# Dense experts in block products: three engines in a fixed order, weights split a pass ahead, GpSimd left out

## The chip, the cores and the metric

One core of a Trainium2 chip runs the whole program. The metric is the time of one execution in microseconds of the device; the median of several runs is compared.

## The reference

Three layers follow each other, all in float32: attention with the queries averaged in pairs, a mixture of 4 dense experts weighted by given probabilities, and a mixture of 8 experts of which each token takes the best one.

```python
def _attn_ref(q, k, v):            # q, k, v: 2 x 8 x 1152 x 64
    q_pool = q.reshape(B, H, S // 2, 2, D).mean(axis=3)
    scores = scale * np.matmul(q_pool, k.transpose(0, 1, 3, 2))
    attn = np.exp(scores - np.max(scores, axis=-1, keepdims=True))
    attn = attn / (np.sum(attn, axis=-1, keepdims=True) + 1e-09)
    return np.matmul(attn, v)
def _moe_ref(x, domain_probs, w1, w2):   # x: 1152 x 512, w1: 4 x 512 x 1024
    p = domain_probs / (domain_probs.sum(-1, keepdims=True) + 1e-09)
    for e in range(E):
        h = np.maximum(x @ w1[e], 0.0)
        out += p[:, e:e + 1] * (h @ w2[e])
def _moe2_ref(x, expert_emb, tau, w1, w2):   # w1: 8 x 512 x 1024
    logits = xn @ en.T / tau                 # x and expert_emb normalised
    expert_idx = np.argmax(logits, axis=1)
    ...
        h = np.maximum(x[mask] @ w1[e], 0.0)
        out[mask] = gate_w[mask, None] * (h @ w2[e])
```

## The kernel before, in words

**Attention** (`attention`, L10 to L236) works through 16 jobs (8 pairs of heads, two parts of the 576 pooled queries each). All its engines follow the order in which the code issues (`tc.manual_schedule()`): scores (L120) and row maxima (matmul L89, VectorE L90, joined at L103), exponentials on ScalarE (L123), sums on GpSimd (L149), the product with v (L155) and the norms (L161 to L172). The first steps (L173 to L188) load k, q and v, and ScalarE issues the loads of v for job 0 itself (L46).

**The dense experts** (`moe1`, L287 to L387) run in eight passes: two halves of 576 tokens (g), four experts (e) each. Every matrix is held as a high part and a remainder, and each product is made of three matmuls. A pass has two phases:

- *Up.* The 512 x 1024 matrix w1 is taken in four units j. A unit multiplies blocks in seven products instead of eight: `unit_w` (L300) loads 512 KB of weights in four pieces, casts 768 columns (ScalarE L308, remainder VectorE L309), forms sums of the blocks with four additions (GpSimd L311 to L314, VectorE for the first two units), and casts 1024 more (L315, L316). The 42 matmuls of a unit, of 288 columns each, go to two kinds of PSUM banks: `ps` collects products one after the other and is copied by ScalarE (`c`, `u`, L334) between them, `py` holds the others (`p` is its copy). VectorE adds (L347, L357), GpSimd adds `u3` (L350), and then ScalarE's relu makes `hh` and VectorE its remainder `hl` (L352, L353).
- *Down.* w2 comes in four pieces of 256 rows, split in high part and remainder (L250, L253). Eight banks (four column blocks d, two groups of tokens of 256 and 320) of 24 matmuls each (L377 to L379) go over `hh` and `hl` of the eight blocks f; VectorE scales the bank by the expert's weight (`prow`), and GpSimd (VectorE for the last expert) adds it to y (L381 to L385).

The order of TensorE in the up phase is that of the code (`manual_schedule` for it alone, L361). All else in `moe1` is placed by the scheduler. `x_sums` (L262) forms the block sums of a half's tokens: for the first half within the last attention jobs, for the second after the up phase of pass 3. The **router** handles ten blocks of tokens (`after`; L484 to L514) whose matmuls use one bank `lr` and one bank `X`; the blocks of each half come at its last expert, two token groups apart (`late`, `flush`). Tables from its counts (matmuls L580, L582) direct the gathers of the routed experts.

**The routed experts** (`moe2`) follow; their weights use buffers of all the pools, and their first matmuls (L700 to L702) stand beside the router's second part.

Of the kernel before, what the change touches and what calls it, by code (L numbers as in the profile page):

```python
# [9 lines left out]
def attention(tc, q, k, v, yr, combos, identF, cc, rp, emb, tau, NJ=16):  # L10

    nc=tc.nc
# [5 lines left out]
    with ExitStack() as ctx:  # L18
# [157 lines left out]
        with tc.manual_schedule():  # L176
# [13 lines left out]
            cb=combos(0,lambda: E1()[:,0:576].rearrange("p (i n) -> p i n",i=2))  # L190
            for g in range(NG):
# [46 lines left out]
NT=10  # L238
# [23 lines left out]
def x_sums(nc, raw, X, tmp):  # L262

    V=nc.vector
    P1,P23,T12,T43=X
    L=[]
    for a in range(2):
        x0,x1=raw[a][:,0],raw[a][:,1]
        lo,hi=slice(0,288),slice(288,576)
        t={}  # L270
        def sub(z,i,i0,i1,t=t):
            def f():
                if z not in t: t[z]=tmp()
                V.tensor_tensor(out=t[z][:,i],in0=i0(),in1=i1(),op=ALU.subtract)
            L.append(f)
        sub(0,0,lambda x0=x0: x0[:,hi],lambda x0=x0: x0[:,lo])
        sub(1,1,lambda x1=x1: x1[:,hi],lambda x0=x0: x0[:,hi])
        sub(0,1,lambda x1=x1: x1[:,hi],lambda t=t: t[0][:,0])
        sub(1,0,lambda x1=x1: x1[:,lo],lambda t=t: t[0][:,1])
        def parts(z,src):  # L280
            L.append(lambda a=a: nc.scalar.copy(z[:,0,a],src()))
            L.append(lambda a=a: V.tensor_tensor(out=z[:,1,a],in0=src(),in1=z[:,0,a].bitcast(F32),op=ALU.subtract))
        parts(T12,lambda t=t: t[0]); parts(T43,lambda t=t: t[1])
        parts(P23,lambda x1=x1: x1.rearrange("p (i n) -> p i n",i=2)); parts(P1,lambda x0=x0: x0[:,lo].rearrange("p (i n) -> p i n",i=1))
    return L

def moe1(tc, pools, ring, hp, tp, psM, psY, yr, X, prow, w1, w2, after, third):  # L287
    nc=tc.nc
    V,G=nc.vector,nc.gpsimd
    ET=mybir.EngineType  # L290
    E=w1.shape[0]
# [4 lines left out]
    late=[]  # L296
    def flush():
        for t in late: after(t)
        late.clear()
    def unit_w(e,j,first):  # L300
# [17 lines left out]
        return [at(wr,0),at(wr,2),at(ws,3),at(wr,1),at(ws,2),at(ws,1),at(ws,0)]  # L318
    for g in range(2):
        for e in range(E):  # L320
            pr=prow(g,e)
            WU=[unit_w(e,j,g==0 and e==0 and j<2) for j in range(4)]
            W2=[load_w(nc,pools,[ring],w2_piece(w2[e],i),('A','V')) for i in range(4)]
            hh=[None]*8; hl=[None]*8
            S=[{} for _ in range(4)]
            def mm(j,i,bank,start,part=(0,6)):
                W=WU[j][i]; z,c=XB[i]
                L=[(W[0][a],z[:,0,a,c]) if m==0 else (W[0][a],z[:,1,a,c]) if m==1 else (W[1][a],z[:,0,a,c]) for a in range(2) for m in range(3)]
                for n,(l,r) in list(enumerate(L))[part[0]:part[1]]:
                    nc.tensor.matmul(bank,l,r,start=start and n==0,stop=n==5,skip_group_check=True)  # L330
            def keep(j,nm,bank):
                if nm=="p1": S[j]['c']=tp.tile([128,2,N],F32,name="c1"); S[j][nm],S[j]["u2"]=S[j]['c'][:,0],S[j]['c'][:,1]
                elif nm!="u2": S[j][nm]=tp.tile([128,N],F32,name=nm)
                nc.scalar.copy(S[j][nm],bank)  # L334
            def p1(j):
                S[j]['X']=psM.tile([128,512],F32,name="ps")[:,0:N]
                mm(j,0,S[j]['X'],True); keep(j,"p1",S[j]['X'])
                for f in (j,j+4):
                    hh[f]=hp.tile([128,576],F32R,name=f"hh{f}"); hl[f]=hp.tile([128,576],F32R,name=f"hl{f}")
            def p5(j):  # L340
                S[j]['Y']=psY.tile([128,512],F32,name="py")[:,0:N]
                mm(j,4,S[j]['Y'],True); keep(j,"p5",S[j]['Y'])
            def p6(j): mm(j,5,S[j]['X'],False); keep(j,"u2",S[j]['X'])
            def p2(j):
                z=psY.tile([128,512],F32,name="py")[:,0:N]
                mm(j,1,z,True)
                V.tensor_tensor(out=S[j]["p1"],in0=z,in1=S[j]["p1"],op=ALU.add)  # L347
            def p7(j):
                mm(j,6,S[j]['X'],False); keep(j,"u3",S[j]['X'])
                G.tensor_tensor(out=S[j]["u3"],in0=S[j]["u3"],in1=S[j]["p5"],op=ALU.add)  # L350
            def low(f,src,cs):
                nc.scalar.activation(out=hh[f][:,cs],in_=src,func=AF.Relu)  # L352
                V.scalar_tensor_tensor(out=hl[f][:,cs],in0=src,scalar=0.0,in1=hh[f][:,cs].bitcast(F32),op0=ALU.max,op1=ALU.subtract)  # L353
# [582 lines left out]
```

## Time and profile before

| | |
|---|---|
| median of 3 runs | 884.47 us (883.15 to 884.5) |
| the profiled execution | 885.35 us, its span 883.6 us |
| mean clock of TensorE | 0.974 of full speed |
| busy: TensorE, VectorE, ScalarE, GpSimd | 803.8, 535.1, 420.5, 393.8 us |

The span is split by stages: attention until about 250.5 us, the eight passes until 729.4, the routed experts until the end. Pass 0 lasts from 250.5 to 317.3, pass 1 to 374.1, pass 2 to 431.7, passes 3 and 4 to 555.9, pass 5 to 612.9, pass 6 to 671.0, pass 7 to 729.4. The share of busy time is a mean over these; which wait ends last is read in each.

### The profile page before, as it was taken

The page shows a single profiled execution, that of the slowest core. Times are in us where ns is not written, and L with a number is a line of the kernel's source. Part 1 is how long each engine was busy: PE and PEld are TensorE (multiplying, and loading weights), DVE is VectorE, ACT ScalarE, POOL GpSimd, SP SyncE. Part 2 cuts the span into 40 slices and gives each one's busy share as a digit, 9 for nine tenths or more (in the row PEclk, how much of TensorE's full clock was granted, in tenths as well). Part 3 has the DMA queues.
Part 4 walks back from the last instruction along what each step waited for, and adds up shares of the span by engine and source line. Part 5 has one row for each costly group of instructions (what it writes and reads, how often), then busy time and mean ns, then how long its engine had stood idle before and what let it go on. Part 6 is the DMA issues. An engine that isn't in the chain of part 4 may idle for free. (4 is left out here: it accounts for less than half of the span.)

```text
span 883.6 us, 16136 instructions
## 1 busy us (share of the span) xinstructions
PE 803.8 (91%) x6067; PEld 700.3 (79%) x6067; DVE 535.1 (61%) x1065; ACT 420.5 (48%) x916; POOL 393.8 (45%) x385
## 2 busy tenths in 40 slices
PE   5999999899967988989889989899798999999996
PEld 3777787677647988978888888889798998877854
DVE  4688888888486346264377565653535848673404
ACT  3466676575745145162273550631614725572524
POOL 4599999878714315355323242353343111330111
PEclk9999999999998999999999999999999999999998
DMA  8532123200044132051231431421313418697991
GB/s 236 143 85 65 27 81 84 29 1 1 2 122 120 49 113 92 3 155 49 68 113 49 120 102 38 133 72 52 106 49 97 154 56 274 236 362 273 394 345 37
DMA packets 101110, 101.32 MB, mean 115 GB/s; under 512 B 28914, under 2 KB 71958, under 8 KB 101024
## 3 DMA queue, kind: packets, MB, share of 16 engines
q1 hardware_dynamic: 97472, 93.71, 33.9%
q0 software_dynamic: 1760, 5.25, 1.7%
q10 hardware_dynamic: 1792, 1.26, 0.5%
q8 instruction: 49, 0.80, 0.4%
q14 instruction: 37, 0.30, 0.1%
HBM read 95.46 MB, written 5.26 MB: 114 GB/s over the span
## 5 line engine op out<-in xcount | busy, mean ns | idle before, releaser
L149 POOL TENSOR_TENSOR es<-es,E 128x512 f32<-128x512 f32 (+1 forms) x108 | 152.9, 1416 | 18.4 <-ACT E L123 10.4
L377 PE MATMUL ps<-hh,w 128*128 128x320 f32 (+1 forms) x512 | 153.3, 301 | 4.0 <-ACT hh L352 4.0
L378 PE MATMUL ps<-hl,w 128*128 128x320 f32 (+1 forms) x512 | 153.8, 300 | 1.5 <-DVE hl L353 1.5
L379 PE MATMUL ps<-hh,w 128*128 128x320 f32 (+1 forms) x512 | 153.2, 300 | 0.0
L330 PE MATMUL ps<-xb,w 128*128 128x288 f32 x576 | 101.8, 314 | 31.5 <-ACT c L334 24.1
L330 PEld LDWEIGHTS ps<-xb,w 128*128 128x128 f32 x576 | 85.7, 199 | 40.4 <-ACT c L334 30.1
L315 ACT CAST w<-st 128x1024 fp32r<-128x1024 f32 x32 | 33.4, 1047 | 173.8 <-issue 130.2
L123 ACT ACTIVATE E<-S 128x320 f32<-128x320 f32 (+1 forms) x288 | 99.7, 411 | 26.4 <-PE S L120 15.6
L330 PE MATMUL py<-xb,w 128*128 128x288 f32 x576 | 99.4, 308 | 11.9 <-ACT w L315 5.9
L377 PEld LDWEIGHTS ps<-hh,w 128*128 128x128 f32 x512 | 98.2, 192 | 4.7 <-ACT hh L352 4.7
L378 PEld LDWEIGHTS ps<-hl,w 128*128 128x128 f32 x512 | 98.4, 192 | 2.4 <-DVE hl L353 2.4
L379 PEld LDWEIGHTS ps<-hh,w 128*128 128x128 f32 x512 | 98.5, 193 | 0.0
L330 PEld LDWEIGHTS py<-xb,w 128*128 128x128 f32 x576 | 86.9, 199 | 14.5 <-ACT p L334 6.5
L253 DVE TENSOR_TENSOR w<-st,w 128x1024 fp32r<-128x1024 f32 x65 | 83.9, 1307 | 23.5 <-ACT w L250 23.0
L90 DVE TENSOR_REDUCE m<-T 128x1 f32<-128x384 f32 x180 | 89.0, 550 | 14.3 <-PE T L89 13.1
L120 PE MATMUL S<-qh,kh 64*128 64x320 f32 (+1 forms) x288 | 86.3, 340 | 1.7 <-ACT E L123 1.7
L120 PE MATMUL S<-qh,kl 64*128 64x320 f32 (+1 forms) x288 | 81.7, 312 | 0.0
L120 PE MATMUL S<-mr,ones 64*128 64x320 f32 (+1 forms) x288 | 78.8, 304 | 0.0
L120 PE MATMUL S<-ql,kh 64*128 64x320 f32 (+1 forms) x288 | 78.3, 305 | 0.0
L155 PE MATMUL O<-E,vn 128*64 128x320 f32 (+1 forms) x576 | 75.7, 409 | 0.0
L250 ACT CAST w<-st 128x1024 fp32r<-128x1024 f32 x65 | 67.5, 1049 | 15.7 <-DMA st<-in_moe_w 8.6
L311 POOL TENSOR_TENSOR st<-st 128x256 f32<-128x256 f32 x30 | 24.4, 814 | 106.1 <-DVE w L309 104.0
(405 smaller groups left out, 1791.8 us busy)
## 6 DMA issues: line engine op xcount, KB each, us to landing
st<-in_moe_w SPq DMA_DIRECT2D x112, 512.0 KB, 5.2
st<-in_moe_w SPq DMA_DIRECT2D x128, 128.0 KB, 3.0
kn<-in_k SPq DMA_DIRECT2D x14, 288.0 KB, 5.0
vn<-in_v SPq DMA_DIRECT2D x14, 288.0 KB, 3.3
qn<-in_q SPq DMA_DIRECT2D x14, 256.0 KB, 4.0
prow<-psc SPq DMA_DIRECT2D x8, 288.0 KB, 4.0
ysc<-ys SPq DMA_DIRECT2D x8, 256.0 KB, 2.1
qn<-in_q SPq DMA_DIRECT2D x14, 64.0 KB, 4.0
```

Source lines behind the costliest of these rows:

```text
L90: nc.vector.tensor_reduce(out=m[:,t,h,c:c+1],in_=s,axis=AX.X,op=ALU.max)
L120: nc.tensor.matmul(s,l[hd],r[hd],start=i==0,stop=i==3)
L123: nc.scalar.activation(out=st['E',g,c][:,h,0:n],in_=s,func=AF.Exp)
L149: nc.gpsimd.tensor_tensor(out=s,in0=st['E',g,0][:,:,0:n] if c==1 else s,in1=st['E',g,c][:,:,0:n],op=ALU.add)
L155: for h in range(2): nc.tensor.matmul(O[HD[h],0:n],vn[:,h,c],st['E',g,c][:,h,0:n],start=c==0,stop=c==NC-1)
L250: if he=='A': nc.scalar.copy(wh,st)
L253: (nc.vector if le=='V' else nc.gpsimd).tensor_tensor(out=wl,in0=st,in1=wh.bitcast(F32),op=ALU.subtract)
L315: nc.scalar.copy(ws[:,0],raw)
L330: nc.tensor.matmul(bank,l,r,start=start and n==0,stop=n==5,skip_group_check=True)
L377: nc.tensor.matmul(po,wh[:,cs],hh[f][:,os],start=(i==0),stop=False)
L378: nc.tensor.matmul(po,wh[:,cs],hl[f][:,os],start=False,stop=False)
L379: nc.tensor.matmul(po,wl[:,cs],hh[f][:,os],start=False,stop=(i==7))
```

## The change

In `moe1` the order of ScalarE and VectorE now follows the code too (`fixed()`), in both phases. The weights of the next pass's units are split in the down phase: `f0` (cast of 768, its remainder, four additions) behind the first bank of each pair, `f1` (cast of 1024, its remainder) behind the second. w2 is loaded and split by column quarters (`down_w`), one in each unit of the up phase. All additions that GpSimd did go to VectorE, but for the four of a unit in the down phase of pass 3, into which the sums of the second half (`x_sums`, now 18 steps in place of 24) are spread. The blocks of the router for the first half are emitted behind pass 3, all five together. The down matmuls take the blocks f in the order 0, 4, 1, 5, 2, 6, 7, 3. The splits of pass 0 are in a fixed order of their own. Some of the pools are allocated ahead of attention; the routed experts have 14 weight buffers in place of 13 and 4 extra stage buffers in place of 5.

```diff
 def moe1(tc, pools, ring, hp, tp, psM, psY, yr, X, prow, w1, w2, after, third):
...
+    fixed=lambda: tc.manual_schedule(engines={ET.PE,ET.Activation,ET.DVE})
...
-    late=[]
-    def flush():
-        for t in late: after(t)
-        late.clear()
-    def unit_w(e,j,first):
+    ORD=[(g,e) for g in range(2) for e in range(E)]
+    WU={}; WD={}
+    def unit_w(n,j,A=V):
...
-        nc.scalar.copy(wr[:,0],raw[:,256:1024])
-        V.tensor_tensor(out=wr[:,1],in0=raw[:,256:1024],in1=wr[:,0].bitcast(F32),op=ALU.subtract)
-        A=V if first else G
-        A.tensor_tensor(out=q[2],in0=q[0],in1=q[2],op=ALU.add)
...
-        nc.scalar.copy(ws[:,0],raw)
-        V.tensor_tensor(out=ws[:,1],in0=raw,in1=ws[:,0].bitcast(F32),op=ALU.subtract)
...
+        def f0():
+            nc.scalar.copy(wr[:,0],raw[:,256:1024])
+            V.tensor_tensor(out=wr[:,1],in0=raw[:,256:1024],in1=wr[:,0].bitcast(F32),op=ALU.subtract)
+            A.tensor_tensor(out=q[2],in0=q[0],in1=q[2],op=ALU.add)
...
+        def f1():
+            nc.scalar.copy(ws[:,0],raw)
+            V.tensor_tensor(out=ws[:,1],in0=raw,in1=ws[:,0].bitcast(F32),op=ALU.subtract)
+        return f0,f1
+    def down_w(n,d):
...
+        nc.sync.dma_start(st.rearrange("p (f c) -> p f c",f=8),w2[e].rearrange("(f p) (d c) -> d p f c",p=128,c=128)[d])
+        w=ring().rearrange("p (l n) -> p l n",l=2)
+        nc.scalar.copy(w[:,0],st)
+        V.tensor_tensor(out=w[:,1],in0=st,in1=w[:,0].bitcast(F32),op=ALU.subtract)
...
-            W2=[load_w(nc,pools,[ring],w2_piece(w2[e],i),('A','V')) for i in range(4)]
...
-                G.tensor_tensor(out=S[j]["u3"],in0=S[j]["u3"],in1=S[j]["p5"],op=ALU.add)
...
-            with tc.manual_schedule(engines={ET.PE}):
...
+        with fixed():
+            for j in range(4):
+                if j==0: p1(0)
...
+                mm(j,4,s['Y'],True); nc.scalar.copy(s['p'],s['Y'])
+                mm(j,5,s['X'],False); nc.scalar.copy(c[:,1],s['X'])
+                if j: out(c21(j-1))
+                down_w(n,j)
...
+                mm(j,1,z,True); V.tensor_tensor(out=c[:,0],in0=z,in1=c[:,0],op=ALU.add)
+                mm(j,2,s['Y'],False,(0,3))
+                mm(j,6,s['X'],False); nc.scalar.copy(s['u'],s['X'])
+                V.tensor_tensor(out=s['u'],in0=s['u'],in1=s['p'],op=ALU.add)
+                if j: out(c1x(j-1))
+                mm(j,2,s['Y'],False,(3,6)); V.tensor_tensor(out=c[:,1],in0=s['Y'],in1=c[:,1],op=ALU.add)
+                if j<3: p1(j+1)
+                else: out(c1x(j))
+                out(c22(j-1 if j<3 else j)) if j else None
+                if j==3: out(c22(2))
+                mm(j,3,s['X'],False)
+            out(c21(3))
...
-                    fs=(0,1,2,4,5,6,3,7)
...
-                        (V if e==E-1 else G).tensor_tensor(out=y,in0=y,in1=t,op=ALU.add)
...
+            for i,f in enumerate((0,4,1,5,2,6,7,3)):
...
+                V.tensor_tensor(out=y,in0=y,in1=t,op=ALU.add)
...
+        with fixed():
+            for i in range(8):
+                d,k=divmod(i,2)
+                bank(d,*PART[g][k])
+                if k==0: pend=unit_w(n+1,d,G if xs else V)
+                pend[k]()
+                for f in xs[i*9//4:(i+1)*9//4]: f()
+        if e==E-1:
+            for t in tiles(0,576): after(t)
+    with fixed():
+        for j in range(4):
+            for f in unit_w(0,j): f()
+    for n in range(len(ORD)): one(n)
...
+            rg=[c2.enter_context(tc.tile_pool(name="ring0",bufs=3,**R,**TW))]
+            sg=[c2.enter_context(tc.tile_pool(name="stage0",bufs=3,**R,**TW))]
             attention(tc,q,k,v,yr,lambda g,tmp: x_sums(nc,yr[g],X,tmp),identF,cc,rp,emb,tau)
...
+            rg.append(c2.enter_context(tc.tile_pool(name="ring1",bufs=6,**R,**TW)))
+            sg.append(c2.enter_context(tc.tile_pool(name="stage1",bufs=1,**R,**TW)))
...
-        sx=c2.enter_context(tc.tile_pool(name="stx",bufs=5,**TW))
...
+        sx=c2.enter_context(tc.tile_pool(name="stx",bufs=4,**TW))
```

How the order moves, at three places.

ScalarE at the start, ahead of job 0. Before (`mr` is the copy of the maxima, `E` the exponentials):

```order
L437 ACTIVATE E,n_243<-E 8x512
L46 DMA vn<-in_v 128x576 x2
L110 CAST mr_277<-T 128x256
L123 ACTIVATE E<-S_287 128x256
L123 ACTIVATE E<-S_289 128x256
L123 ACTIVATE E<-S_313 128x256
```

Now:

```order
L463 ACTIVATE E,n_247<-E 8x512
L46 DMA vn<-in_v 128x576 x2
L310 CAST w<-st 128x768
L110 CAST mr_281<-T 128x256
L317 CAST w<-st 128x1024
L310 CAST w<-st 128x768
L123 ACTIVATE E<-S_294 128x256
L123 ACTIVATE E<-S_296 128x256
```

Three casts of weights stand around the copy of the maxima, ahead of the first exponential. On VectorE a unit's subtractions and additions stand ahead of the maxima of the next job in the same way. Behind attention, VectorE's splits of units 1 to 3 stand in one piece ahead of unit 0's first addition.

ScalarE in an up phase, pass 1. Before (`w` from `st` is a weight cast; `c1`, `p5`, `u3` are copies of PSUM banks):

```order
L352 ACTIVATE hh0_4610<-u3_4647 128x288
L352 ACTIVATE hh4_4612<-c1_4608 128x576
L250 CAST w_4586<-st_4584 128x1024
L334 COPY c1_4665<-ps_4658 128x288
L352 ACTIVATE hh0_4610<-ps_4601 128x288
L334 COPY p5_4686<-py_4679 128x288
L334 COPY c1_4665<-ps_4658 128x288
L334 COPY u3_4712<-ps_4658 128x288
L250 CAST w_4596<-st_4594 128x1024
L352 ACTIVATE hh1_4667<-u3_4712 128x288
L352 ACTIVATE hh5_4669<-c1_4665 128x576
L334 COPY c1_4730<-ps_4723 128x288
```

Now:

```order
L364 COPY u3_4659<-ps_4638 128x288
L346 ACTIVATE hh4_4584<-c1_4581 128x576
L345 COPY c1_4707<-ps_4706 128x288
L346 ACTIVATE hh0_4582<-u3_4595 128x288
L357 COPY p5_4728<-py_4727 128x288
L358 COPY c1_4707<-ps_4706 128x288
L346 ACTIVATE hh1_4640<-ps_4638 128x288
L325 CAST w_4748<-st_4746 128x1024
L364 COPY u3_4729<-ps_4706 128x288
L346 ACTIVATE hh5_4642<-c1_4639 128x576
```

The copies come in the order in which the matmuls make them, with one cast (L325, w2) per unit between them; of the next pass's units only one cast of 768 stands in an up phase, ahead of unit 2 or 3.

TensorE and the router's blocks for the first half. Before, in the down phase of pass 3 (`lr`, `X` are the router's banks, L377 to L379 the down matmuls):

```order
L486 MATMUL X<-identF,y_103 128x128
L377 MATMUL ps<-hh_5748,w 128x320
L378 MATMUL ps<-hl_5749,w 128x320
L379 MATMUL ps<-hh_5748,w 128x320
L377 MATMUL ps<-hh_5805,w 128x320
L378 MATMUL ps<-hl_5806,w 128x320
L484 MATMUL lr<-enT,y_103 128x8
L486 MATMUL X<-identF,y_103 128x128
L379 MATMUL ps<-hh_5805,w 128x320
```

Now, in the up phase of pass 4 (L339 is the up matmul):

```order
L510 MATMUL lr<-enT,y_102 128x8 x4
L512 MATMUL X<-identF,y_102 128x128 x4
L339 MATMUL ps<-xc_101,w 128x288
L512 MATMUL X<-identF,y_102 128x128 x4
L339 MATMUL ps<-xc_101,w 128x288 x5
L339 MATMUL py<-xb_98,w 128x288
L524 LDWEIGHTS ones
L524 MATMUL lr<-oh,ones 128x8
L525 LDWEIGHTS low
L525 MATMUL lr<-oh,low 128x8
L339 MATMUL py<-xb_98,w 128x288 x4
L510 MATMUL lr<-enT,y_102 128x8 x4
```

The blocks moved out of pass 3's down phase, all five to the first 60 up matmuls of pass 4. At the other end of the program, between the last down bank and the first table of the router's second part, 36 matmuls of the routed experts' first layer stand now, and 136 matmuls of the routed experts before.

## Rows read from the trace of the kernel before

**Rows 1.** Busy time by stretch (columns: stretch, its us, busy us of each engine, clock, DMA):
```profile
250.50:317.30 66.80, 53.93 (x359) 51.16 (x357) 37.78 (x59) 25.68 (x47) 18.53 (x20) 0.90 0.33 96
317.30:431.70 114.40, 102.19 (x723) 99.32 (x722) 54.95 (x81) 43.48 (x80) 48.48 (x55) 0.97 0.27 80
431.70:555.90 124.20, 110.95 (x802) 106.99 (x802) 78.58 (x213) 55.01 (x113) 40.02 (x53) 0.96 0.29 87
555.90:671.00 115.10, 103.20 (x727) 99.62 (x726) 54.68 (x81) 44.40 (x82) 48.50 (x55) 0.97 0.27 79
671.00:729.40 58.40, 55.15 (x415) 53.09 (x413) 39.15 (x89) 29.46 (x58) 12.80 (x16) 1.00 0.36 116
374.10:401.10 27.00, 23.00 (x164) 21.70 (x163) 19.01 (x26) 17.32 (x34) 13.19 (x14) 1.00 0.54 148
347.60:374.10 26.50, 26.50 (x200) 26.41 (x199) 8.36 (x14) 4.36 (x8) 9.21 (x12) 1.00 0.08 28
697.60:729.40 31.80, 31.80 (x250) 31.15 (x248) 19.68 (x61) 12.53 (x26) 3.20 (x7) 1.00 0.29 95
729.40:883.60 154.20, 143.16 (x871) 112.05 (x870) 79.21 (x186) 72.96 (x113) 26.48 (x23) 0.97 0.76 275
```

**Rows 2.** Waits of TensorE over the whole span: total us, times, longest:
```profile
PE ps L330 <- ACT c L334: 24.1, 18, 3.1
```

**Rows 3.** Timeline of TensorE, start of pass 2's up phase (start us, us, engine, line):
```profile
374.06 0.96 PE L330 MATMUL ps<-xc,w 128*128 128x288 f32 x6
374.86 0.95 PE L330 MATMUL py<-xb,w 128*128 128x288 f32 x6
```

**Rows 4.** Groups by shape, pass 5's up phase 555.9 to 582.3:
```profile
L253 DVE TENSOR_TENSOR w<-st,w 128x1024 fp32r<-128x1024 f32 x4 | 5.9, 1508 | 0.3 <-ACT w L250 0.3
...
L316 DVE TENSOR_TENSOR w<-st,w 128x1024 fp32r<-128x1024 f32 x3 | 3.7, 1225 | 4.1 <-ACT w L315 4.1
...
L309 DVE TENSOR_TENSOR w<-st,w 128x768 fp32r<-128x768 f32 x3 | 2.9, 955 | 0.3 <-ACT w L308 0.3
...
L353 DVE SCALAR_TENSOR_TENSOR hl<-c,hh 128x576 fp32r<-128x576 f32 x3 | 2.8, 933 | 0.0
...
L347 DVE TENSOR_TENSOR c<-py,c 128x288 f32<-128x288 f32 x4 | 1.8, 450 | 1.8 <-PE py L330 1.8
...
L250 ACT CAST w<-st 128x1024 fp32r<-128x1024 f32 x4 | 4.2, 1043 | 0.0
...
L334 ACT COPY c<-ps 128x288 f32<-128x288 f32 x8 | 3.2, 398 | 0.8 <-PE ps L330 0.7
...
L312 POOL TENSOR_TENSOR st<-st 128x256 f32<-128x256 f32 x3 | 2.6, 870 | 0.2
```

**Rows 5.** Timeline of the start, 13 to 20 us:
```profile
14.61 1.68 ACTq L46 DMA_DIRECT2D vn<-in_v  x2
...
17.03 0.15 DVE L103 TENSOR_REDUCE MM<-m 128x4 f32<-128x12 f32 x1
...
19.17 0.66 ACT L123 ACTIVATE E<-S 128x256 f32<-128x256 f32 x2 [0.78 <-PE S L120]
...
19.49 1.02 DVE L90 TENSOR_REDUCE m<-T 128x1 f32<-128x384 f32 x2 [2.31 <-PE T L89]
```

**Rows 6.** Timeline around the start of pass 0, 246 to 266 us:
```profile
248.58 1.99 ACT L315 CAST w<-st 128x1024 fp32r<-128x1024 f32 x2 [4.70 <-POOL st L314]
...
260.10 0.41 DVE L312 TENSOR_TENSOR st<-st 128x256 f32<-128x256 f32 x1
...
265.21 0.85 PE L330 MATMUL py<-xb,w 128*128 128x288 f32 x2 [5.86 <-ACT w L315]
```

**Rows 7.** Timeline of TensorE in the second router part, 713 to 754 us:
```profile
717.17 0.96 PE L484 MATMUL lr<-enT,y 128*128 128x8 f32 x8
...
720.05 0.96 PE L484 MATMUL lr<-enT,y 128*128 128x8 f32 x8
...
753.18 0.40 PE L580 MATMUL X<-dAm,Bm 128*128 128x30 bf16 x10
```

More of the change, by code (lines that the diff above doesn't have):

```diff
@@ L230, in attention @@
                         av(g,3,NC); norm(g,0)
-                if g>NG//2:
-                    for f in cb[:4]: f()
-                    del cb[:4]
+                if g>=NG//2:
+                    m=2+(g>=NG-2)
+                    for f in cb[:m]: f()
+                    del cb[:m]
             g=NG-1
@@ L265, in x_sums, with sub, f, parts @@
     P1,P23,T12,T43=X
-    L=[]
[L267 to L284, printed above, removed]
+    x=raw.rearrange("p (a k) (i n) -> p k i a n",k=2,i=2)
+    t={}
+    L=[]
+    def sub(n,i0,i1):
+        def f():
+            t[n]=tmp()
+            V.tensor_tensor(out=t[n],in0=i0(),in1=i1(),op=ALU.subtract)
+        return f
+    def parts(z,src):
+        return [lambda: nc.scalar.copy(z[:,0],src()),lambda: V.tensor_tensor(out=z[:,1],in0=src(),in1=z[:,0].bitcast(F32),op=ALU.subtract)]
+    xa=lambda k,i: (lambda: x[:,k,i])
+    ta=lambda n: (lambda: t[n])
+    h1,l1=parts(T12[:,:,0],ta(1)); h2,l2=parts(T12[:,:,1],ta(2)); h4,l4=parts(T43[:,:,0],ta(4)); h3,l3=parts(T43[:,:,1],ta(3))
+    L+=[sub(1,xa(0,1),xa(0,0)),h1,sub(2,xa(1,1),ta(1)),l1,h2,sub(4,xa(1,0),ta(2)),l2,h4,sub(3,xa(1,1),xa(0,1)),l4,h3,l3]
+    for z,k,i in ((P23[:,:,0],1,0),(P23[:,:,1],1,1),(P1[:,:,0],0,0)): L+=parts(z,xa(k,i))
     return L
@@ L389 @@
+    with fixed():
+        for j in range(4):
+            for f in unit_w(0,j): f()
+    for n in range(len(ORD)): one(n)
 NE,NE1=4,3
@@ L481, in block @@
         ts=slice(t,t+1)
-        yt=[yr[g][dc//2][:,dc%2,o:o+n] for dc in range(4)]
+        yt=[yr[g][:,dc,o:o+n] for dc in range(4)]
         lg=psX.tile([128,8],F32,name="lr")[0:n]
@@ L538, in third @@
     def third():
-        two=itertools.cycle([al['x0'],lambda: al['m'](0)])
-        x01=x_parts(nc,psX,"X",dict(x=lambda: next(two)()),res['xs'],2,identF)
+        two=iter([al['x0'](),al['m'](0)])
+        x01=x_parts(nc,psX,"X",dict(x=lambda: next(two)),res['xs'],2,identF)
         x3,x3p=al['xs3']()
@@ L885, in prow @@
             def prow(g,e):
-                r=pp.tile([128,576],F32,name="prow",bufs=2)
+                r=pp.tile([128,576],F32,name="prow")
                 nc.sync.dma_start(r,psc[e:e+1,g*576:(g+1)*576].to_broadcast([128,576]))
@@ L905, in attn_moe_moe_kernel @@
         xm.append(c2.enter_context(tc.tile_pool(name="xm",bufs=1,**TW)))
[L906 to L907 removed]
+        sx=c2.enter_context(tc.tile_pool(name="stx",bufs=4,**TW))
+        pools['stage']=turns((*sg,sx),(3,1,4),[128,1024],F32,"st",[sg[0]]*3+[sg[1]])
         xp=c2.enter_context(tc.tile_pool(name="xp2",bufs=2,**TW))
[L909 to L910 removed]
+        Y=[lambda dt=F32R,b=b: yp.tile([128,2048],dt,name=f"y{b}") for b in range(2)]
         A=ring
         X=[lambda dt=F32R,b=b: xTp.tile([128,2048],dt,name=f"xb{b}") for b in range(3)]
[L913 removed]
+        rings=[A,X[1],X[2],A,A,A,A,A,Y[1],X[0],A,A,Y[0],A]
         pools['n']=0
```

160 lines of the change are left out of this document (72 added, 88 removed).

## The prediction

> **What bounds the kernel now.** I read three views in this order: the stretches pass by pass, the waits of TensorE, and the groups of one up phase. The stretches [rows 1] show four parts: attention to 250.5 us, eight passes of the dense experts to 729.4, and the routed experts for the last 154.2. The change touches mostly the passes. Four of them (1, 2, 5, 6) are alike: 114.4 + 115.1 = 229.5 us, 57.4 each. TensorE is the engine that matters in them, but it isn't always fed. In a run without a gap, six matmuls of 288 columns start 0.80 us after the six before them [rows 3], so 168 matmuls of an up phase would take 22.4 us; pass 2 took 27.0 [rows 1]. The down phase of pass 1 took 26.5 without an idle moment. A pass could thus last about 49 us, and lasts 57.4. The difference is idle time in the up phases and a clock of 0.97 around them.
>
> The view of waits says whose fault it is: 24.1 us in 18 waits of up-phase matmuls for ScalarE's copy `c` [rows 2]. The copy itself lasts 0.398 [rows 4]; what makes it late is the engine's order, in which a weight cast of 1.04 us or an activation that waits for GpSimd stands ahead of it. GpSimd needs 0.87 us for an addition [rows 4] that VectorE does in 0.41 [rows 6].
>
> **The sum, part by part** (us; durations from [rows 4] unless said).
>
> *Start: +3.2.* The first weight casts now stand in ScalarE's list ahead of job 0. The cast can't start before the `vn` issues end at 14.61 + 1.68 = 16.29 [rows 5]. A cast of 768 columns (some 0.83, by the 1.043 of one of 1024), the subtraction of 0.96, an addition of 0.41 [rows 6] and about 0.6 of small steps that stood there already bring the row maxima of L103 from 17.03 to 19.1. Behind them the 1.04 cast waits for three more additions (to 20.4, then 21.4), and the next unit's cast follows; the first exp moves from 19.17 to about 22.3. On VectorE the subtraction of 1.23 behind that cast moves the next L90 from 19.49 to 22.7. Attention has one fixed order on all engines, so I let the whole shift through. Bounds: +2 (only the L103 delay) and +4.5 (a late DMA).
>
> *Pass 0: -4.0.* Before, TensorE stood 5.86 us until 265.21 for a cast of unit 1 [rows 6]; the pass ended at 317.3, 52.1 us later, for some 16 us of up-phase matmuls and 26.5 of a down phase, with a clock of 0.90 over the pass [rows 1]. Now the attention norms no longer queue behind two casts at 248.58 [rows 6], which starts VectorE's splitting about 3 us sooner. But the splits of units 1 to 3 stand in one piece ahead of the additions of unit 0: per unit 0.96 + 4 x 0.41 + 1.04 + 1.23 = 4.9, two units, and a subtraction at each end, 12.3 in all. From about 253.5 that ends near 265, as late as before. After it 16.8 us of up-phase matmuls, about 5 of tail and slow clock and 26.5 for the down phase end the pass at 313.3, were it not for the shift of the start. Bounds: 0 and -6.
>
> *Passes 1, 2, 5, 6: -20.7.* One unit of the up phase is 42 matmuls, 5.6 us. ScalarE then has one cast (1.04), four copies and two activations of 288 columns (about 0.40 each) and one activation of 576 (some 0.7, by its columns): 4.2 in all. VectorE has 1.23 for the weights, 0.75 (estimated from its columns) to 0.93 for the 576-column remainder, and five of 0.45: 4.2 to 4.4. Both fit in 5.6. The tightest place is the third PSUM bank of `py`: the product z of unit j+1 needs the addition of unit j, and by my count of the rows VectorE reaches it 0.1 us ahead. At the end of unit 3 the order leaves two remainders late. Its w2 cast ends some 3.65 us into the unit; behind it VectorE has 1.23, 0.45, 0.45, the remainder of unit 2 (0.75) and 0.45, then ScalarE activates (0.7), and hl7 is there at about 8.5, hl3 after three more short ones at 9.9. Bank 0 reaches hl7 at 7.0 and, after that wait of 1.5, hl3 at 8.9: 2.5 us per pass. In the down phase VectorE has 5.65 us per two banks (0.96 + 1.64 + 1.23 for the unit, four of about 0.45 for y) against 6.4 of matmuls. So a pass is 22.4 + 2.5 + 25.6 + 0.9 between the phases + 0.8 for slips and clock = 52.2, and four are 208.8 against 229.5. Bounds: 50.5 each (-27.5) and 55 each (-9.5).
>
> The longer of the two VectorE values is what stands while GpSimd is busy: two subtractions of the same form take 1.508 and 1.225 in one stretch [rows 4]. The Trainium skill (SBUF — State Buffer, section "SBUF: two separate sides") says that VectorE and GpSimd share a port pair, which one instruction holds to its end while the other is blocked; by that, with GpSimd silent, the short values hold everywhere. If the long ones stayed, the margin of 0.1 us would turn into some 0.25 per two units, 0.5 us a pass, and the sum would end 2 us higher.
>
> *Passes 3 and 4: -2.* Before 124.2, which is 9.4 over two ordinary passes, for the sums of the second half and five router blocks. Ordinary passes now give 104.4. In pass 3 the four additions per unit stay on GpSimd (4 x 0.87, then ScalarE 1.04, then VectorE 1.23 in its fixed place): a chain of 8 to 9 us per two banks against 6.4, of which three PSUM banks take up about 5 us in all. I add 4, and 3 for VectorE's remainders ahead of pass 4. The router now runs wholly in the up phase of pass 4. Where blocks came closest their first matmuls were 2.9 us apart [rows 7]; with VectorE's other work between, I take 3.5, so 17.5 us for five blocks, with 60 up matmuls (8 us) inside them: 9.5 more, and 1 for the tables. 104.4 + 4 + 3 + 10.5 = 122. Bounds: -9 (blocks at 2.9 and nothing in pass 3) and +8 (blocks at 5).
>
> *Pass 7: -1.5.* Its up phase had about 4 us to lose and gets the 2.5 tail; the down phase is full of TensorE work [rows 1] and stays. Bounds -3 and +1.
>
> *Routed experts: +4.5.* The list of TensorE now has 36 first-layer matmuls (some 8 us) between the last down bank and the tables of the second router part; before, 136 stood there. The tables came 23.8 us after the last bank, at 753.2 [rows 7], because VectorE had the router to finish; freed of the remainders that stood in it, I take 17 to 18. So TensorE is idle about 9 us. The whole stretch has 154.2 - 143.2 = 11 us idle, with DMA at 0.76 on average [rows 1], so some of it comes back later as less waiting for weights; I take half. Bounds 0 and +11.
>
> The attention's fewer subtractions, the prefetched rings, w2 in column quarters and the single `prow` buffer cost nothing in the sum: weights are asked for a whole phase ahead, and VectorE and SyncE aren't on attention's path. If that cover went, rival C shows the price.
>
> Sum: +3.2 - 4.0 - 20.7 - 2 - 1.5 + 4.5 = -20.5. The profiled execution took 885.35 us, so 864.85; it lies 0.88 over the median of the runs, which makes **864.0**.
>
> **Rivals.** A, *VectorE becomes the bound*: all additions of the unit go to it, and its load per pass rises from about 27 us [rows 1] to about 40. If the count at the `py` bank is off by a few tenths, the passes last about 55, and the time is 864.0 + 11.2 = 875.2. For it: the margin of 0.1. Against it: 40 of 52 us still leaves room.
>
> B, *more comes back*: passes at 50.5, start +2, pass 0 -6, passes 3 and 4 -7, pass 7 -2.5, the end 0. That is -41 and 843.5. For it: fewer gaps should lift the clock from 0.97. Against it: every term at its good end.
>
> C, *slower: fixed order locks ScalarE and VectorE in step*. Each now waits in its own list for the other: cast before subtraction before addition before activation. If a late weight or copy heads one list, all behind it stands. Wholly in step a unit would take 4.2 + 4.4 = 8.6 us instead of 5.6; with 32 units it decides from 20.5 / 32 = 0.64 us per unit, a fifth of the way. At 0.9 a unit (a third) the time is 864.0 + 28.8 = 892.8. For it: exactly such a wait, VectorE and then TensorE behind one cast, cost 5.86 us in pass 0 [rows 6]. Against it: by the count above each list has over 1 us to spare per unit. The Trainium skill (PSUM — Partial Sum Buffer, section "Engine vs sequencer instructions") calls these engines' queues strictly first in, first out; the row agrees, and the rule is what would make C so dear.
>
> That the change does nothing is excluded by the lists: the orders differ.
>
> **How the numbers follow.** My forecast 0.55 (857 to 872), A 0.18 (872 to 882), B 0.14 (843 to 857), C 0.10 (886 and more), no net effect 0.03. The range of 848 to 880 leaves out C, the rest of A above 880, and B's end: under 2 in 10. A change of 0.2% (1.8 us) is about what a measurement of this kernel can tell. Faster: 0.55 + 0.18 + 0.14 = 0.87; within: 0.03; slower: 0.10.
>
> **What would show it.** Right: passes 1, 2, 5, 6 near 52, waits for `c` nearly gone, a wait for hl of about 2.5 us at each down phase's start, first exp 3 us later, TensorE idle some 9 us behind the last pass. Wrong: waits of `py` on VectorE's addition in every unit (A), ScalarE and VectorE waiting for each other throughout (C), or pass 4 above 75 us.

## The result and the profile after

The change takes 873.83 us (median of 4 runs, 870.48 to 876.67) against 884.49: a ratio of 0.988, with an interval of 0.9835 to 0.9925. It is 10.7 us faster, where 20.5 were forecast. The profiled execution took 876.11 us, its span 874.3.

Busy time by stretch after (stretch, its us, busy us of TensorE, its weight loads, VectorE, ScalarE and GpSimd, clock, DMA share, GB/s), cut as in [rows 1]:

```profile
251.20:313.40 62.20, 51.30 (x359) 50.35 (x357) 44.05 (x79) 25.91 (x46) 0.00 (x0) 0.89 0.36 99
313.40:413.20 99.80, 98.03 (x722) 96.37 (x721) 74.39 (x135) 44.12 (x80) 0.00 (x0) 1.00 0.32 91
413.20:543.40 130.20, 115.56 (x805) 112.22 (x804) 84.74 (x233) 56.52 (x113) 21.30 (x28) 0.90 0.28 83
543.40:645.20 101.80, 97.91 (x722) 96.07 (x721) 73.95 (x135) 43.99 (x80) 0.00 (x0) 1.00 0.31 89
645.20:702.80 57.60, 54.73 (x415) 53.14 (x414) 39.57 (x95) 29.74 (x58) 4.01 (x7) 1.00 0.34 108
702.80:874.30 171.50, 145.56 (x872) 114.13 (x871) 80.87 (x185) 72.73 (x113) 22.26 (x23) 0.93 0.69 250
```

| stretch | before | after | difference | forecast |
|---|---|---|---|---|
| start to pass 0 | 250.5 | 251.2 | +0.7 | +3.2 |
| pass 0 | 66.8 | 62.2 | -4.6 | -4.0 |
| passes 1, 2, 5, 6 | 229.5 | 201.6 | -27.9 | -20.7 |
| passes 3 and 4 | 124.2 | 130.2 | +6.0 | -2 |
| pass 7 | 58.4 | 57.6 | -0.8 | -1.5 |
| routed experts | 154.2 | 171.5 | +17.3 | +4.5 |

The ordinary passes last 50 to 51 us, with a clock of 1.00 where it was 0.97. More than 23 of the 28 us are lost again at two places, passes 3 and 4 and the routed experts. The waits of TensorE after (total us, times, longest) show both:

```profile
PE X L606 <- DVE dAm L601: 13.0, 1, 13.0
...
PE ps L339 <- ACT u L364: 10.0, 1, 10.0
...
PE ps L386 <- DVE hl L347: 5.5, 11, 1.1
...
PE ps L339 <- ACT xc L277: 4.8, 1, 4.8
...
PE lr L510 <- DVE y L393: 4.6, 1, 4.6
...
PE ps L339 <- ACT c L345: 2.0, 4, 0.8
```
The 24.1 us for `c` [rows 2] are down to 2.0. What is new are single long waits: 13.0 for the router's tables, 10.0 for the copy `u` in pass 0, and 4.8 and 4.6 between passes 3 and 4. The 5.5 us for `hl` are 11 waits of at most 1.1 us, where the prediction had 2.5 in each pass.

The end of pass 3, from the timeline after (start us, us, engine, line):

```profile
463.05 0.31 PE L387 MATMUL ps<-hh,w 128*128 128x320 f32 x1
...
468.35 0.95 DVE L311 TENSOR_TENSOR w<-st,w 128x768 fp32r<-128x768 f32 x1
...
469.38 1.17 POOL L312 TENSOR_TENSOR st<-st 128x256 f32<-128x256 f32 x1 [4.75 <-DVE w L311]
...
472.36 0.72 POOL L315 TENSOR_TENSOR st<-st 128x256 f32<-128x256 f32 x1
...
473.12 1.04 ACT L317 CAST w<-st 128x1024 fp32r<-128x1024 f32 x1 [5.52 <-POOL st L315]
474.07 0.67 ACT L277 CAST xc<-y 128x576 fp32r<-128x576 f32 x1
474.19 1.23 DVE L318 TENSOR_TENSOR w<-st,w 128x1024 fp32r<-128x1024 f32 x1 [3.29 <-ACT w L317]
...
474.79 0.61 PE L339 MATMUL ps<-xc,w 128*128 128x288 f32 x1 [4.76 <-ACT xc L277]
```
GpSimd's additions start when VectorE has written the remainder (L311), ScalarE's cast behind them waits 5.5 us for GpSimd, and VectorE's next subtraction waits 3.3 us for that cast. The cast of `xc`, which the first up matmul needs, stands behind the same cast in ScalarE's list. The last down matmul had ended at 463.4 (it starts at 463.05 and lasts 0.31); the first up matmul comes at 474.79, 11.4 us later.

The last stretch, in the same view:

```profile
716.65 0.92 ACT L729 ACTIVATE hh<-ps 128x256 fp32r<-128x256 f32 x3
...
723.08 0.45 PE L606 MATMUL X<-dAm,Bm 128*128 128x30 bf16 x10 [13.03 <-DVE dAm L601]
...
724.83 1.08 DVE L730 SCALAR_TENSOR_TENSOR hl<-ps,hh 128x256 fp32r<-128x256 f32 x3
```
Three PSUM banks of first-layer results were full from 710.1 on, when the last of the 36 matmuls ended. ScalarE empties them only from 716.65, and VectorE makes their remainders (L730) at 724.83, behind the whole router.

### The profile page after: what moved, and what is told of

It is laid out like the page before. It is cut to its first block, busy times and chain, and to the rows that moved or that the text cites. A ratio compares the mean times of both kernels' runs of the same rounds, so it can differ in the third digit from the quotient of the medians.

```text
span 874.3 us, 16001 instructions
## 1 busy us (share of the span) xinstructions
PE 795.0 (91%) x6067; PEld 697.7 (80%) x6067; DVE 591.0 (68%) x1223; ACT 422.2 (48%) x914; POOL 244.2 (28%) x217
## 5 line engine op out<-in xcount | busy, mean ns | idle before, releaser
L123 ACT ACTIVATE E<-S 128x320 f32<-128x320 f32 (+1 forms) x288 | 99.3, 411 | 20.4 <-PE S L120 15.9
L339 PE MATMUL ps<-xb,w 128*128 128x288 f32 x576 | 96.9, 304 | 12.0 <-ACT u L364 10.0
L317 ACT CAST w<-st 128x1024 fp32r<-128x1024 f32 x32 | 33.6, 1049 | 142.1 <-DVE st L315 67.8
L339 PE MATMUL py<-xb,w 128*128 128x288 f32 x576 | 97.7, 305 | 0.0
L90 DVE TENSOR_REDUCE m<-T 128x1 f32<-128x384 f32 x180 | 89.0, 548 | 12.6 <-PE T L89 11.0
L339 PEld LDWEIGHTS ps<-xb,w 128*128 128x128 f32 x576 | 84.1, 193 | 15.0 <-ACT u L364 11.4
L339 PEld LDWEIGHTS py<-xb,w 128*128 128x128 f32 x576 | 85.9, 196 | 0.0
L89 PE MATMUL T<-kh,qh 64*128 64x384 f32 x180 | 62.9, 385 | 4.9 <-DVE m L90 4.5
L312 POOL TENSOR_TENSOR st<-st 128x256 f32<-128x256 f32 x4 | 4.7, 1170 | 214.3 <-DVE w L311 214.3
L120 PEld LDWEIGHTS S<-qh,kh 64*128 64x128 f32 x288 | 52.1, 189 | 13.6 <-issue 7.0
```

Of the source, the lines that this page charges most:

```text
L89: nc.tensor.matmul(s,qh[HD[h],(2*u+t)*128:(2*u+t+1)*128],kh[HD[h],c*384:(c+1)*384],start=True,stop=True)
L90: nc.vector.tensor_reduce(out=m[:,t,h,c:c+1],in_=s,axis=AX.X,op=ALU.max)
L120: nc.tensor.matmul(s,l[hd],r[hd],start=i==0,stop=i==3)
L123: nc.scalar.activation(out=st['E',g,c][:,h,0:n],in_=s,func=AF.Exp)
L339: nc.tensor.matmul(bank,l,r,start=start and m==0,stop=m==5,skip_group_check=True)
```

## Experiments

Times are medians; the kernel before, measured beside them, took 884.3 to 885.0 us (883.5 beside the last run). Where a time has no interval, the kernel was run once. The stretches are read from one trace of each kernel.

**Pass 3 on VectorE.**

```diff
-                if k==0: pend=unit_w(n+1,d,G if xs else V)
+                if k==0: pend=unit_w(n+1,d,V)
```

> One part undone: in the down phase of pass 3 the four additions of a unit go to VectorE as everywhere else, not to GpSimd. Theory 1 (the chain VectorE, GpSimd, ScalarE, VectorE makes the down phase of pass 3 lag): the gap between the last down bank of pass 3 at 463.2 us and the first up matmul of pass 4 at 474.8, 11.6 us, shrinks to some 3 us, and the time falls by 7 to 9 us to about 865. Rival (VectorE has too much to do there, the sums of the second half and the additions alike): its list gets 4 x 4 additions of 0.42 more, the gap stays near 11 us or grows by up to 3, and the time does not move. Either way the other passes keep their 50 to 51 us.

865.17 us (ratio to before 0.977, 0.974 to 0.980), 8.7 less than the change. Passes 3 and 4 and the last stretch in its trace:

```profile
414.40:531.20 116.80, 110.68 (x806) 106.85 (x805) 90.14 (x249) 56.56 (x113) 8.12 (x12) 0.96 0.32 93
690.60:864.50 173.90, 145.38 (x871) 114.08 (x870) 81.07 (x185) 72.69 (x113) 22.62 (x23) 0.93 0.69 246
```
130.2 became 116.8, and the up phase of pass 4 starts 5.8 us behind the last down bank in place of 11.4. The time is theory 1's, but the gap is halved and not down to 3: GpSimd's chain, in a fixed list, made 5.6 us of it, and 5.8 stay without that chain. Of the rest of the 13.4 us, the up phase of pass 4 saved 4.6 (33.6 in place of 38.2) and what follows it 3.2. The last stretch took 2.4 us more.

**Router behind the up phase of pass 4.**

```diff
             out(c21(3))
+        if n==E:
+            for t in range(NT):
+                if TOK[t][0]==0: after(t)
...
-        if e==E-1:
-            for t in tiles(0,576): after(t)
```

> One part undone: the five router blocks of the first half are emitted behind the up phase of pass 4, so that they fall beside down matmuls, which need no ScalarE or VectorE work in between, instead of up matmuls. Theory 1 (what passes 3 and 4 lose is the wait of the fixed lists on router blocks in an up phase that needs all three engines): passes 3 and 4 fall from 130.3 us to about 118, the up phase of pass 4 to 25, the time to about 864. Rival (the 11.6 us gap behind pass 3 is all that matters and has nothing to do with the router): the gap stays, the up phase of pass 4 still starts at about 474.8, and the five blocks cost as much in the down phase as they did in the up phase: no change within 2 us.

867.16 us (0.980, 0.977 to 0.984).

```profile
413.60:534.00 120.40, 108.57 (x801) 105.62 (x801) 81.79 (x230) 56.51 (x112) 19.30 (x27) 0.94 0.28 85
```
Passes 3 and 4 fell by 9.8 us: the up phase of pass 4, to the end of its last matmul, took 26.8 us in place of 38.2, what follows it 32.0 in place of 30.5. The gap of 11.4 us ahead of it stayed. So both theories own a part: the router in the up phase was one cost, GpSimd's chain another.

**The hidden tiles' pool first.**

```diff
+        xp=c2.enter_context(tc.tile_pool(name="xp2",bufs=2,**TW))
         xm.append(c2.enter_context(tc.tile_pool(name="xm",bufs=1,**TW)))
...
-        xp=c2.enter_context(tc.tile_pool(name="xp2",bufs=2,**TW))
```

> One line moved: the pool of the routed experts' hidden tiles (hh2, hl2) is allocated ahead of two others, so that it lies where the dense experts' hidden tiles were and not where the router's scratch is. Theory 1 (the remainders of the first layer stand behind the whole router on VectorE because their memory is the router's; three PSUM banks fill and TensorE stands 13.0 us): the remainders stand among the router's steps again, TensorE does 96 first-layer matmuls ahead of the tables, the wait of 13.0 us becomes 0 to 4, and the time falls by 8 to 13 us to about 863. Rival (the last stretch is bound by the loads of the weights, and the wait only hides that): the idle time comes back later as waits for weights, and the time falls by less than 3 us.

857.96 us (0.969, 0.966 to 0.972), 15.9 less than the change with one line moved.

```profile
702.20:857.80 155.60, 143.30 (x871) 111.86 (x871) 80.72 (x185) 72.35 (x113) 24.89 (x23) 0.98 0.75 276
```
The last stretch is 155.6 us, near the 154.2 before the change, and the 13.0 us wait is gone from its list of waits. In its trace VectorE makes the first remainder among the router's steps, long before the tables:

```profile
706.57 0.41 DVE L730 SCALAR_TENSOR_TENSOR hl<-ps,hh 128x256 fp32r<-128x256 f32 x1
...
722.15 0.31 DVE L601 TENSOR_TENSOR dAm<-A,tk 128x150 bf16<-128x150 f32 x1
```
The tables come as late behind the last bank as in the change, some 20 us in both; TensorE now has first-layer matmuls to do until then. Theory 1 holds, the rival falls: the loads of the weights don't bind here. The new split of the pools had put `hh2` and `hl2` where their instructions had to come after the router. That it is the router's scratch that lay there is read from the order of the pools in the code; no trace shows addresses.

**GpSimd back, order fixed.** `A=V` became `A=G` in `unit_w`, and the additions of u3 and of y (but for the last expert) went to `G`.

> GpSimd is put back for the additions of the units, of u3 and of y, in every pass; the fixed order of the three engines and the splits a pass ahead stay. Theory 1 (the gain of the four ordinary passes comes from the fixed order, and GpSimd out of it is worth little): passes 1, 2, 5, 6 stay at 50 to 53 us. Rival (the gain comes from GpSimd being left out, since its 0.87 us per addition stood in the chain of every unit): the chain VectorE, GpSimd, ScalarE, VectorE of 8 to 9 us per two banks against 6.4 makes each down phase lag as in pass 3, and these passes last 57 to 62 us, the time is 895 or more.

908.41 us.

```profile
315.20:422.70 107.50, 99.52 (x722) 97.88 (x722) 51.97 (x80) 44.06 (x80) 46.21 (x55) 0.98 0.29 83
556.00:668.60 112.60, 101.44 (x722) 99.60 (x721) 50.73 (x79) 43.75 (x80) 47.04 (x54) 0.95 0.28 81
```
The four ordinary passes take 220.1 us, 18.5 more than with VectorE, and there are long waits for `c` again, though one in each of seven passes and not 18 in all:

```profile
PE ps L339 <- ACT c L345: 24.4, 7, 5.5
```
The passes, 55.0 us each, lie between the theories; the time is on the rival's side. A fixed order with GpSimd in it is 9.4 us better in these passes than the kernel before, but 24 us worse in the whole program.

**Order left to the scheduler.** Only TensorE follows the code, as before the change:

```diff
-    fixed=lambda: tc.manual_schedule(engines={ET.PE,ET.Activation,ET.DVE})
+    fixed=lambda: tc.manual_schedule(engines={ET.PE})
```

> One part undone: only TensorE follows the code in the dense experts; where ScalarE's and VectorE's instructions stand is the scheduler's again, in both phases. GpSimd stays left out and the weights stay split at the same places of the code. Theory 1 (order and engines each give a share: with the fixed order and GpSimd back the four ordinary passes took 220 us, against 229.5 before and 201.6 in the change): these passes take between 205 and 225 us, with waits for the copies c and u back in the up phases. Rival (GpSimd left out is all of it, and the order is worth nothing by itself): they take 201 to 203 us and the time stays near 874.

839.84 us: 34 less than the change. Neither theory had this.

```profile
308.80:405.80 97.00, 96.95 (x723) 96.16 (x722) 72.81 (x135) 43.45 (x80) 0.00 (x0) 1.00 0.32 94
405.80:514.50 108.70, 106.12 (x801) 103.15 (x801) 87.28 (x233) 55.24 (x112) 23.43 (x28) 1.00 0.34 100
514.50:611.50 97.00, 97.00 (x723) 96.16 (x722) 73.53 (x135) 43.54 (x80) 0.00 (x0) 1.00 0.32 94
667.20:838.10 170.90, 144.50 (x871) 113.16 (x870) 80.91 (x185) 72.60 (x113) 22.55 (x23) 0.94 0.69 250
```
The four ordinary passes take 194.0 us without an idle moment of TensorE, passes 3 and 4 108.7 in place of 130.2, and pass 0, from its first matmul, 57.2 in place of 62.9. The order by hand cost time in every stretch of the dense experts. The wait of 13.0 us for the tables is still there:

```profile
PE X L606 <- DVE dAm L601: 13.0, 1, 13.0
```

**Splits of pass 0 moved.** Units 2 and 3 are split at the end of units 0 and 1 (`if n==0 and j<2: for f in W0[j]: f()` behind the unit's last product), and no longer ahead of the pass.

> One piece moved: in pass 0 the splits of units 2 and 3 are emitted at the end of units 0 and 1 of the up phase, and not ahead of the pass in one piece. Theory 1 (the 10.0 us wait for the copy u stems from VectorE's splits of three units standing ahead of unit 0's additions): the wait shrinks to 2 to 4 us, VectorE's load then sets the up phase at some 30 us, pass 0 falls from 62.1 to about 58 and the time by 3 to 5 us to about 869. Rival (VectorE is full in this phase wherever the splits stand): the same time is lost unit by unit, and the time does not move by more than 1.5 us.

869.33 us (0.983, 0.978 to 0.987), 4.5 less, though the two intervals overlap. Pass 0, from its first matmul, is 59.1 us, where the change has 62.9 (250.4 to 313.4):

```profile
251.90:311.00 59.10, 52.72 (x364) 51.38 (x363) 44.26 (x80) 26.43 (x47) 0.00 (x0) 0.94 0.38 104
```
The 10.0 us wait is gone; in its place stand two waits for `p`, 5.5 us together. Passes 3 and 4 are 3.2 us shorter in this trace too (127.0), which the edit doesn't explain.

**Three edits together** (pass 3 on VectorE, router late, pool first).

> The three edits that were each faster by themselves together: additions of pass 3 on VectorE, router blocks behind the up phase of pass 4, the pool of the hidden tiles first. If they mend three different places, passes 3 and 4 take some 112 us (50 + 4 + 26 + 32) in place of 130.3, the last stretch some 156 in place of 171.5, and the time is about 843 to 846. Rival (what is saved ahead of the last stretch is lost in it, since the weights of the routed experts come no sooner): the last stretch takes 160 us or more and the time is 850 to 855.

843.45 us (0.953, 0.949 to 0.957). Passes 3 and 4 took 114.0, the last stretch 155.5. The times add up (8.7 + 6.7 + 15.9 = 31.3, measured 30.4). The pool mends a place of its own; the other two overlap in part, since passes 3 and 4 fell by 16.2 us where the two alone took off 13.4 and 9.8.

**And the splits of pass 0.**

> The three edits of the run before and the moved splits of pass 0. If the fourth is independent of them, it is 3 to 5 us faster than the run with three, at about 840; if VectorE is full in pass 0 anyway, it is within 1.5 us of it.

841.53 us (0.952, 0.948 to 0.957), 1.9 less, between the two cases; the intervals overlap, so that it is faster at all is not settled by the times alone. In the traces pass 0 fell by about 4 us (315.0 - 252.0 against 310.0 - 251.1).

**VectorE for GpSimd, and nothing else.** In the kernel before:

```diff
-        A=V if first else G
+        A=V
...
-                G.tensor_tensor(out=S[j]["u3"],in0=S[j]["u3"],in1=S[j]["p5"],op=ALU.add)
+                V.tensor_tensor(out=S[j]["u3"],in0=S[j]["u3"],in1=S[j]["p5"],op=ALU.add)
...
-                        (V if e==E-1 else G).tensor_tensor(out=y,in0=y,in1=t,op=ALU.add)
+                        V.tensor_tensor(out=y,in0=y,in1=t,op=ALU.add)
```

> One part of the change alone: the kernel before, with the additions of the units, of u3 and of y on VectorE in place of GpSimd in the dense experts; order, weights, pools and router as before. Theory 1 (leaving GpSimd out is the largest gain, since an addition on it takes twice as long and stands in the chain of every unit): the ordinary passes fall from 57.4 us to 51 to 54, the time to 850 to 865. Rival (the gain is in where the weights are split, a pass ahead, and GpSimd matters only together with it, as in the run with the fixed order and GpSimd back): these passes stay at 56 us or more and the time above 873.

827.02 us (0.935, 0.932 to 0.939): 58 us less than before, 47 less than the change. It goes further than the change in one point: the additions of pass 4's units are on VectorE too.

```profile
307.30:406.90 99.60, 97.30 (x723) 96.10 (x722) 71.92 (x136) 43.51 (x80) 0.00 (x0) 1.00 0.32 91
406.90:513.00 106.10, 104.75 (x802) 102.61 (x802) 87.69 (x254) 54.68 (x113) 6.95 (x12) 1.00 0.34 102
513.00:614.70 101.70, 98.31 (x726) 96.39 (x725) 72.44 (x136) 44.39 (x82) 0.00 (x0) 1.00 0.32 89
670.60:824.90 154.30, 142.06 (x873) 110.77 (x871) 79.36 (x186) 72.56 (x113) 25.53 (x23) 0.99 0.75 275
```
Its ordinary passes take 201.3 us, the same as in the change, its passes 3 and 4 106.1 and its last stretch 154.3. Theory 1 holds and is surpassed: the ordinary passes give 28 of the 58 us, passes 3 and 4 another 18, pass 0 some 10. The waits for `c`, 24.1 us in [rows 2], go without any change to the order:

```profile
PE ps L330 <- ACT c L334: 3.2, 3, 1.8
```
They named ScalarE, but ScalarE itself had waited for GpSimd. Its waits in passes 1 and 2 of the kernel before:

```profile
ACT hh L352 <- POOL u L350: 6.1, 3, 2.6
ACT w L315 <- POOL st L314: 4.4, 2, 2.5
```
Everything else in the change, with the additions that it left on GpSimd in pass 3, cost 47 us.

**Free order, pool first.** The edits of the free run and of the pool together.

> The run with the order of ScalarE and VectorE left to the scheduler, with the pool of the hidden tiles moved. If the loss in the last stretch is independent of the order of the passes, the wait of 13.0 us for the tables goes as it did before, the last stretch falls from 170.9 to some 155, and the time from 839.8 to 823 to 826. Rival (with the passes shorter the weights of the last stretch come too late): 830 or more.

824.61 us (0.932, 0.928 to 0.935); the last stretch is 156.2. The loss there is independent of the passes.

**Free order, GpSimd back.** The edits of the free run and of the run with GpSimd together.

> The order left to the scheduler as in the run before the last, and GpSimd back for the additions of the units, of u3 and of y; the places of the splits, the column quarters of w2, the pools and the router as in the change. Theory 1 (GpSimd left out is most of the gain in a free order too): the four ordinary passes, 194 us in the free run, rise to 205 to 220 and the time to 855 to 870. Rival (the places of the splits and the quarters are the gain; a free order works round GpSimd's longer additions): they stay below 200 and the time below 848.

864.82 us.

```profile
313.40:418.70 105.30, 100.61 (x722) 97.97 (x721) 54.80 (x80) 42.99 (x80) 43.73 (x55) 0.98 0.30 86
533.10:636.10 103.00, 99.62 (x727) 96.80 (x727) 53.89 (x80) 43.53 (x81) 44.58 (x55) 1.00 0.30 88
```
The ordinary passes take 208.3 us, as theory 1 had it: 14.3 more than without GpSimd, but 21.2 less than before. The rest of the change (the places of the splits, w2 in quarters, the order of the banks) is worth something in a free order as well.

**Free order, pool first, GpSimd out of pass 3 too.**

> What the runs point to: the order of ScalarE and VectorE left to the scheduler, the pool of the hidden tiles first, and now the additions of pass 3 on VectorE too, so that GpSimd is out of every pass. Theory 1 (in a free order the chain over GpSimd in pass 3 still costs a little): passes 3 and 4 fall from 108.7 to some 106, as in the kernel before with VectorE alone, and the time from 824.6 to 821 to 823. Rival (a free order hides that chain, and VectorE has enough to do in pass 3): within 1.5 us of 824.6.

822.40 us (0.930, 0.927 to 0.932; 5 runs). Passes 3 and 4 took 106.3 (406.8 to 513.1). It is 2.2 us under the run with the free order and the pool first; the intervals overlap, so the times alone don't settle that it is faster. In the traces passes 3 and 4 fell by 2.4 us (108.7 there). Its median is the lowest of all that was run.

## Why the prediction was right, and where not

The time lies in the range and the sign is right, but the gain is half of what was forecast, and the range holds only because errors cancel: that part is luck. The ordinary passes came out 7.2 us better than their term, passes 3 and 4 8.0 and the routed experts 12.8 worse; the first and the last of these lie outside the bounds given for them.

*Start.* The first exp moved to 21.82 and L90 to 22.35, as worked out (22.3 and 22.7 against 19.17 and 19.49 in [rows 5]):

```profile
21.82 0.65 ACT L123 ACTIVATE E<-S 128x256 f32<-128x256 f32 x2
...
22.35 1.94 DVE L90 TENSOR_REDUCE m<-T 128x1 f32<-128x384 f32 x4
```
At the end of attention only 0.7 us of it were left. Other runs with this start and without GpSimd in the passes have the first up matmul at 250.1 to 252.0, against 249.7 and 250.3 in the two with the old start, so between nothing and 2.3 us is left, and not 3.2. "I let the whole shift through" failed; where it was made good was not tried.

*Pass 0* came out by its own steps: the copy `u` at the end of three units' splits, and TensorE going on at 266.40, with 265 and the shift of the start in the text.

```profile
266.40 1.81 PE L339 MATMUL ps<-xb,w 128*128 128x288 f32 x6 [10.02 <-ACT u L364]
```
*Passes 1, 2, 5, 6.* The rows' count held: VectorE and ScalarE fit into a unit, the `py` bank never waited, A and C did not come. The term was mis-sized: the tail was 1 us and not 2.5, and the clock stayed at 1.00. What failed is its reason. I put the 24.1 us of waits [rows 2] down to ScalarE's order first, and named GpSimd's slower additions only beside it; so I put the gain down to the fixed order. The runs give these four passes as (one trace each):

| us | GpSimd adds | VectorE adds |
|---|---|---|
| kernel before | 229.5 | 201.3 |
| change, order free | 208.3 | 194.0 |
| change, order fixed | 220.1 | 201.6 |

VectorE in GpSimd's place is worth 28.2, 14.3 or 18.5, the rest of the change (the new places of the splits among it) 21.2 or 7.3, and the fixed order costs 11.8 or 7.6. Two of the three parts gain, the one that I credited loses.

With GpSimd silent, VectorE's own instructions get shorter too. Passes 1 and 2 of the kernel before, then of the same kernel with VectorE in GpSimd's place (count, busy us, mean ns):

```profile
L253 DVE TENSOR_TENSOR w<-st,w 128x1024 fp32r<-128x1024 f32 x8 | 10.8, 1365 | 1.5 <-ACT w L250 1.5
...
L353 DVE SCALAR_TENSOR_TENSOR hl<-c,hh 128x576 fp32r<-128x576 f32 x8 | 7.3, 911 | 0.2
```
```profile
L253 DVE TENSOR_TENSOR w<-st,w 128x1024 fp32r<-128x1024 f32 x9 | 10.9, 1220 | 0.4 <-ACT w L250 0.3
...
L353 DVE SCALAR_TENSOR_TENSOR hl<-c,hh 128x576 fp32r<-128x576 f32 x11 | 8.3, 752 | 0.0
```
The weights' subtraction fell from 1365 to 1220 ns and the remainder of 576 columns from 911 to 752. The Trainium skill (SBUF — State Buffer, section "SBUF: two separate sides") has one of the two engines blocked while the other holds the shared ports; the rows agree. Both sides pay: in the kernel before, the remainder at 327.84, with GpSimd idle, takes 0.75 us, and the one at 342.31, beside which GpSimd's addition at 342.89 falls, 1.12; that addition takes 1.13, and one with VectorE out of its way 0.74 (at 319.78). An addition on GpSimd thus costs more than its own 0.87 us. But these two rows make 8 x 0.145 + 8 x 0.159 = 2.4 us of VectorE's time in two passes that got 14.8 us shorter, so by this estimate the blocking of VectorE is the smaller part, and the additions' place in ScalarE's chain the larger; no run separates the two.

*Passes 3 and 4.* The chain over GpSimd was seen, but the 7 us for it ("I add 4, and 3") became a gap of 11.4, of which 5.6 go with GpSimd; the up phase of pass 4 took 38.2 us where 35.4 were in the sum, and the first gather added a wait of 3.1 in its down phase. The cover that I counted on, three PSUM banks, held: TensorE waits for no bank in the down phase of pass 3. The lag comes out behind the last bank, as the waits for `y` (4.6) and `xc` (4.8). Pass 4 took 68.7 us from its first up matmul and 80 with that gap, so the sign "pass 4 above 75 us" falls between. The free order hides most of this: 108.7 with the same additions on GpSimd.

*Routed experts.* This step failed most: 17.3 in place of 4.5. I read the cause off TensorE's list (36 matmuls ahead of the tables) and took half of 9 us back as fewer waits for weights. The tables came 20.3 us behind the last bank, where I took 17 to 18, so the wait was 13.0, and nothing came back. Behind it the matmuls ran at the lower clock:

```profile
702.80:710.00 7.20, 7.20 (x64) 6.80 (x63) 4.83 (x28) 3.92 (x10) 0.79 (x2) 1.00 0.87 299
710.00:723.00 13.00, 0.06 (x1) 0.00 (x0) 12.93 (x73) 4.18 (x9) 2.32 (x3) 0.61 0.92 319
723.00:729.70 6.70, 5.38 (x40) 5.17 (x41) 3.18 (x16) 0.38 (x1) 0.95 (x1) 0.50 0.16 56
729.90:735.00 5.10, 5.10 (x43) 5.05 (x42) 1.27 (x3) 1.38 (x4) 0.00 (x0) 1.00 0.00 0
```
The cause of the short list was one step further: memory. The pool that moved shows it, since with it the stretch falls by 15.9 us, to within 2 us of the 154.2 of before, although the tables come no sooner behind the last bank.

*Rival C* was half right. A fixed list does hold up what stands behind a wait, as the Trainium skill has it for these queues (PSUM — Partial Sum Buffer, section "Engine vs sequencer instructions"), but here it did so in pass 0, pass 3 and the router's blocks in pass 4, where the code's order wasn't the order in which data came, and not unit by unit: in the ordinary passes TensorE's waits stand at the start of a phase, 5.7 us in all. The wait for the second router part is no case of it, since it stayed in the free order.

## What to carry to other kernels

A wait that names one engine may be another's slowness: replace the slow engine in the kernel as it is, and measure that alone, before the order is rewritten. An order fixed by hand must be compared against the scheduler's order with the same instructions: here it paid in no stretch of the dense experts, cost least where the loop repeats in step (7.6 us in four passes) and most at its ends (21.5 in passes 3 and 4), where routers, sums and loads come in. When pools are moved, look at whose memory a stage inherits, since its first writes wait for the last reader.

## What was not expected of the hardware

VectorE took over all additions, worked 37 us in a pass in place of 27, and the passes got shorter. A pause of TensorE cost more than its length: 13.0 us of wait were followed by 6.7 us at a granted clock of 0.50, which is the lower of the two levels (1.2 GHz), while the 5 us after them were at 1.00. Before the wait TensorE had been busy without a gap, at 1.00. The stretch fell by 15.9 us when the wait of 13.0 went.
